# Computing an attention denominator from Gram sums of the key features, ahead of the numerator, in a fused linear-attention and FFN kernel

## Chip, cores and metric

One Trainium2 chip, one core of it. The metric is the device time in microseconds (us) of one launch. A run is called slow where it is over 1.5% above the fastest of the same kernel; comparisons below use fast runs, and where a run was slow the text says so.

Engine names in the profile: PE is TensorE (matmuls), PEld its weight loads, DVE is VectorE, ACT is ScalarE, POOL is GpSimd, SP is SyncE, which only issues DMAs here. SPq is SyncE's in-order queue of DMA issues.

## The reference

```python
# q, k, v: 4 batches x 4 heads x 1088 tokens x 32;  S1, S2: 8 x 32
def phi(x):                       # 64 features of a token: all products a_i * b_j
    a = einsum('rd,bhsd->bhsr', S1, x)
    b = einsum('rd,bhsd->bhsr', S2, x)
    return einsum('bhsi,bhsj->bhsij', a, b).reshape(..., 64)
q_p, k_p = phi(q), phi(k)
kv  = einsum('bhsf,bhsd->bhfd', k_p, v)
z   = sum(k_p, axis=2)
num = einsum('bhsf,bhfd->bhsd', q_p, kv)
den = einsum('bhsf,bhf->bhs', q_p, z)[..., None] + 1e-6
attn = num / den
x = attn.transpose(0, 2, 1, 3).reshape(4352, 128)      # 4 heads x 32 = 128 columns
h = maximum(x @ w_in, 0)                               # w_in: 128 x 2048
out = (h * h) @ w_out                                  # w_out: 2048 x 128
```

The point of the change: since phi is made of products, z is an 8 x 8 matrix, the Gram sum of a and b over the keys, and den = a_q' Z b_q. The denominator of a token needs only its 8 a-features and the 8 rows y = Z b_q (in this kernel the roles of a and b are laid out by the shuffles), not its 64 products.

## The kernel before

Tokens are handled in chunks: three per batch (384, 384 and 320 tokens), 12 in all. While TensorE runs the FFN of one chunk (16 steps: a matmul in f16 to 128 of the 2048 hidden columns, and an f32 matmul back, which the trace shows as two records), the other engines prepare the next chunk's attention. A small planner, run while the kernel is built, puts every attention task at one FFN step of one engine; the engines then run their instructions in exactly that order.

```python
def a_qg(b, ch):              # a and b features of q, packed 64x32 tiles
    for r in range(2):
        for o in range(4):
            nc.tensor.matmul(qg[32*o:32*o+32, 512*r : 512*r+n], sqn[...], qT[...])

def a_sh(b, ch, s, i):        # VectorE: spread features over partitions, 4 per chunk
    nc.vector.stream_shuffle(in_=qg..., out=t_..., mask=mask_q[s][i])

def a_qpn(b, ch, s):          # GpSimd: products of the features, read by a_ndn as they lie
    nc.gpsimd.tensor_tensor(out=qp, in0=sh0, in1=sh1, op=mult)

def a_ndn(b, ch):             # numerator (i = 0) and denominator (i = 1) rows
    for i in range(2):
        for g in range(2):
            for h in range(H):
                nc.tensor.matmul(nd[32*h:32*h+32, 512*g + 192*i : ... + n],
                                 kw[64*g:64*g+64, 128*i + 32*h : ... + 32],
                                 qpn[h % 2][64*g:64*g+64, c0 : c0 + n])
# then on VectorE, per chunk: a_dT (transpose of den), a_rd (reciprocal of 12 columns),
# a_rb (transpose back), a_x (num * 1/den); then ScalarE a_ax, TensorE a_sum,
# VectorE rs and s2 (a power-of-two scale per token), GpSimd a_xs -> xT, input of the FFN

class _Plan:
    LAG = {"PE": 2, "DVE": 1, "ACT": 1, "POOL": 1, "SP": 1}
    def add(self, key, eng, dur, needs, f, *args, ...):
        s = first
        for k in needs:
            s = max(s, self.at[k] + self.LAG[eng])     # steps after what it needs
        # ... then the first step with room on that engine; dur is an estimate in us
```

The FFN's own elementwise work (ReLU `gt`/`g` and squares `g`) is spread over ScalarE, VectorE and GpSimd by a balance that fills what the plan leaves free.

## Time and profile before

| | before |
|---|---|
| median of 4 runs | 194.94 us (194.86 to 195.44) |
| span of the profiled run | 193.2 us |
| TensorE busy | 185.9 us, 96% |
| VectorE / ScalarE / GpSimd busy | 122.8 / 138.1 / 94.7 us |

The page's first part: busy time of each engine, its share of the span, and its instructions.

```profile
span 193.2 us, 4586 instructions
PE 185.9 (96%) x1666; PEld 111.2 (58%) x1666; DVE 122.8 (64%) x316; ACT 138.1 (71%) x338; POOL 94.7 (49%) x158
```

The list of waits of TensorE before: engine and line, what it waited for, us in total, how many times, the longest.

```profile
PE warm L877 <- DVE zero L160: 1.2, 1, 1.2
PE pg L725 <- ACT xT L697: 0.3, 1, 0.3
PE xp L688 <- DVE xs L663: 0.3, 2, 0.2
PE pg L725 <- ACT gt L735: 0.2, 1, 0.2
```

All of that lies in the prologue, and it is about 2 us in sum. TensorE bounds the kernel, and what attention costs is the time that its matmul groups take between FFN steps. One such group, from the timeline of TensorE before (start us, duration, engine, line, operation, form, count):

```profile
94.39 0.70 PE L756 MATMUL po<-g,w_o 128*128 128x320 f32 x2
95.02 0.88 PE L472 MATMUL ndn<-qp,kw 64*32 64x192 f32 x32
95.69 0.53 PE L441 MATMUL qg<-qT,sqn 64*32 64x192 f32 x16
96.16 0.31 PE L725 MATMUL pg<-xT,w_in 128*128 128x320 f16 x1
```

Ends are modelled and overlap, so read starts. The FFN step in front of this group starts at 94.25, and a plain step of this chunk takes 0.675 us, so without the group the next step would have started at 94.93; it started at 96.16. The group costs 1.23 us. In this is a late start of the packed group of about 0.09 us (95.02 instead of 94.93).

### The profile page before, as it was taken

Reading aid. Unit: us, or ns where it says so; the run is one execution under the profiler, and the core shown is the slowest. Engines: PE = TensorE matmul, PEld = TensorE weight load, DVE = VectorE, ACT = ScalarE, POOL = GpSimd, SP = SyncE. Lnnn points to the kernel's source line nnn. Section 1 sums busy time; section 2 is a strip of 40 time slices with the busy share of each in tenths; the row PEclk is TensorE's granted clock in tenths of the full one; section 3 lists DMA queues with packets and bytes.
Section 4 is the critical chain, followed back from the end, with each engine's and each line's share of the span. In section 5 each row is a group of like instructions: output and inputs, shape, how many; then the busy total and the mean of one; then the engine's idle time right before and its main releaser. Section 6 shows DMA issues by size and latency. Waiting matters only on the chain.

```text
span 193.2 us, 4586 instructions
## 1 busy us (share of the span) xinstructions
PE 185.9 (96%) x1666; PEld 111.2 (58%) x1666; DVE 122.8 (64%) x316; ACT 138.1 (71%) x338; POOL 94.7 (49%) x158
## 2 busy tenths in 40 slices
PE   7998999999999999999999999999999999999990
PEld 2673655456656555456666555556566555556990
DVE  3958876974586763964566674873666665547740
ACT  3326695895496996996498896896596896867740
POOL 5833484955325382984346363984245371630000
PEclk9999999999999999999999999999999999999997
DMA  5699340020085100020157200010110200200201
GB/s 163 177 289 299 88 142 5 0 41 3 12 204 155 43 11 3 11 33 3 17 154 210 38 6 3 14 29 3 25 19 2 34 3 0 41 2 0 44 0 34
DMA packets 27344, 11.40 MB, mean 59 GB/s; under 512 B 19194, under 2 KB 26042, under 8 KB 27322
## 3 DMA queue, kind: packets, MB, share of 16 engines
q1 hardware_dynamic: 27174, 11.05, 23.5%
q8 instruction: 13, 0.21, 0.5%
q10 hardware_dynamic: 148, 0.07, 0.1%
q14 instruction: 9, 0.07, 0.1%
HBM read 8.78 MB, written 2.23 MB: 57 GB/s over the span
## 4 chain that ended last, share of the span: by engine, by line
PE 93%; DVE 2%; ACT 2%; issue 0%; DVEq 0%; ACTq 0%
PE po L756 58%; PE pg L725 16%; PE ndn L472 4%; PE kvp L338 2%; PE warm L877 2%; PE qg L441 2%; PE pt L773 2%; PE nd L595 2%; PE rep L901 1%; PE kvp L352 1%; PE sm L522 1%; PE kf L381 1%; PE kf L280 1%; ACT gt L735 1%; ACT g L719 1%
## 5 line engine op out<-in xcount | busy, mean ns | idle before, releaser
L756 PE MATMUL po<-g,w_o 128*128 128x384 f32 (+3 forms) x386 | 144.0, 459 | 0.0
L719 ACT ACTIVATE g<-gt 128x384 f32<-128x384 f32 (+1 forms) x164 | 80.7, 503 | 7.7 <-DVE gt L737 7.1
L735 ACT ACTIVATE gt<-pg 128x384 f32<-128x384 f32 (+2 forms) x137 | 64.6, 474 | 28.6 <-PE pg L725 27.9
L756 PEld LDWEIGHTS po<-g,w_o 128*128 128x128 f32 x386 | 65.9, 190 | 32.7 <-ACT g L719 18.7
L725 PE MATMUL pg<-xT,w_in 128*128 128x384 f16 (+2 forms) x193 | 60.9, 317 | 0.7 <-ACT xT L697 0.3
L737 DVE TENSOR_SCALAR gt<-pg 128x384 f32<-128x384 f32 (+1 forms) x56 | 29.4, 524 | 34.4 <-PE pg L725 27.9
L746 POOL TENSOR_TENSOR g<-gt 128x384 f32<-128x384 f32 (+1 forms) x26 | 20.7, 801 | 49.0 <-ACT gt L735 49.0
L725 PEld LDWEIGHTS <-w_in 128*128 128x128 f16 x193 | 18.9, 98 | 24.4 <-issue 6.8
L459 POOL TENSOR_TENSOR qp<-sh 128x384 f32<-128x384 f32 (+1 forms) x20 | 18.8, 948 | 7.9 <-DVE sh L450 7.9
L450 DVE STREAM_SHUFFLE sh<-qg 128x384 f32<-128x384 f32 (+1 forms) x40 | 20.4, 563 | 0.0
L546 POOL TENSOR_TENSOR xT<-x,rs 128x384 f16<-128x384 f32 (+1 forms) x10 | 9.5, 952 | 6.2 <-DVE rs L537 6.0
L306 POOL TENSOR_TENSOR kp<-fs 128x1152 f32<-128x1152 f32 x3 | 9.5, 3169 | 5.0 <-DVE fs L299 5.0
L537 DVE TENSOR_SCALAR rs<-sm 128x384 uint32<-128x384 uint32 (+1 forms) x10 | 5.3, 527 | 7.9 <-PE sm L522 7.9
L482 DVE STREAM_TRANSPOSE dT<-ndn 128x384 f32<-128x384 f32 (+1 forms) x10 | 5.5, 548 | 7.0 <-PE ndn L472 7.0
L788 POOL COPY br<-beta 32x3 f32<-32x3 f32 x32 | 5.9, 183 | 6.4 <-DVE beta L678 5.1
L472 PE MATMUL ndn<-qp,kw 64*32 64x192 f32 (+1 forms) x320 | 8.4, 318 | 0.0
L555 POOL TENSOR_TENSOR bt<-s 128x384 f32<-128x384 f32 (+1 forms) x10 | 7.9, 786 | 0.0
L472 PEld LDWEIGHTS ndn<-qp,kw 64*32 64x32 f32 x320 | 4.7, 106 | 4.9 <-issue 3.9
L364 POOL TENSOR_TENSOR ks<-kp 128x1024 f32<-128x1024 f32 x3 | 7.1, 2365 | 0.2
L877 PE MATMUL warm<-zero 128*128 128x512 f16 x16 | 5.7, 521 | 1.2 <-DVE zero L160 1.2
L338 PEld LDWEIGHTS kvp<-kp,vn 128*32 128x32 f32 x288 | 4.8, 110 | 2.7 <-issue 2.2
L274 DVE STREAM_TRANSPOSE qT<-qn 128x384 f32<-128x384 f32 (+1 forms) x12 | 6.3, 535 | 0.0
(119 smaller groups left out, 154.9 us busy)
## 6 DMA issues: line engine op xcount, KB each, us to landing
vn<-in_v_dram SPq DMA_DIRECT2D x32, 64.0 KB, 3.9
kn<-in_k_dram SPq DMA_DIRECT2D x3, 544.0 KB, 11.9
qn<-in_q_dram SPq DMA_DIRECT2D x3, 544.0 KB, 3.3
out_dram<-oT SPq DMA_DIRECT2D x24, 48.0 KB, 1.8
w_in<-in_moe_w_in_dram SPq DMA_DIRECT2D x2, 512.0 KB, 9.0
w_o<-in_moe_w_out_dram SPq DMA_DIRECT2D x2, 512.0 KB, 11.1
out_dram<-oT SPq DMA_DIRECT2D x12, 40.0 KB, 1.7
qn<-in_q_dram SPq DMA_DIRECT2D x2, 192.0 KB, 3.8
```

Of the source, the lines that this page charges most:

```text
L306: (nc.vector if g == 0 else nc.gpsimd).tensor_tensor(out=_ap(st[b, "kp2"], 0, 128, 128 * NT * g, [[64, 2 * NT], [8, 8], [1, 8]]), in0=_ap( ...
L450: nc.vector.stream_shuffle(in_=_ap(st[b, "qg", ch], 0, 128, 0, [[512, 2], [1, n]]), out=_ap(t_, 0, 128, 0, [[n, 2], [1, n]]), mask=mask_q[ ...
L459: nc.gpsimd.tensor_tensor(out=qp[:, 0 : 2 * n], in0=st[b, "sh", ch, s, 0][:, 0 : 2 * n], in1=st[b, "sh", ch, s, 1][:, 0 : 2 * n], op=mult,)
L472: nc.tensor.matmul(nd[32 * h : 32 * h + 32, 512 * g + 192 * i : 512 * g + 192 * i + n], st[b, "kw"][64 * g : 64 * g + 64, 128 * i + 32 * h ...
L546: nc.gpsimd.tensor_tensor(out=st[b, "xT"][:, 384 * ch : 384 * ch + n], in0=st[b, "x", ch][:, 0:n], in1=st[b, "rs", ch][:, 0:n], op=mult,)
L719: nc.scalar.activation(dst, src, Square)
L725: nc.tensor.matmul(pg[:, c0:c1], w_in[:, 128 * c : 128 * c + 128], st[b, "xT"][:, 384 * ch + c0 : 384 * ch + c1],)
L735: nc.scalar.activation(gt[:, c0:c1], pg[:, c0:c1], Relu)
L737: nc.vector.tensor_scalar(out=gt[:, c0:c1], in0=pg[:, c0:c1], scalar1=0.0, scalar2=None, op0=amax)
L746: (nc.vector if on[1] == "DVE" else nc.gpsimd).tensor_tensor(out=g2[:, c0:c1], in0=gt[:, c0:c1], in1=gt[:, c0:c1], op=mult)
L756: nc.tensor.matmul(st["po", b, ch][:, c0:c1], w_o[:, 128 * c : 128 * c + 128], g2s[i][1][:, c0:c1], start=first, stop=(c == NFF - 1), skip ...
L877: nc.tensor.matmul(t_[:, 0:512], zero[:, 0:128], zero[:, :])
```

## The change

Intent: take the denominator rows out of `ndn` (half its matmul records), replace the z matmuls (16 records of 64 columns a batch) by shorter Gram records (18 of 32 columns), and fold 1/den into the q features, so that the nd2 matmul gives x directly and the VectorE chain behind it (dT, rd, rb, x) goes. The feature order that the Gram form needs is not the order in which nd2 must read the products, so six SBUF-to-SBUF DMAs per chunk (`mv`) move them. Batch 0 keeps the old form; batches 1 to 3 (nine chunks) use the new one. Names below: nd2 is the new numerator group (tile `ndn`), qgy the matmuls of the q features and y rows (tile `qk`), kf those of the key features, kvp the group that sums over the keys; `xT` is the input of the FFN, `gt` its ReLU, `g` its square, and `xs`, `rs`, `s` the scaling of x. The core of the diff:

```diff
+    def a_gram(b, t):                       # 32-column Gram records instead of z
+        nc.tensor.matmul(kvp[32*(t%4):..., 64:96], fs[.. odd ..], fs[.. even ..], ...)
+    def a_qgy(b, ch, qg):                   # q features and y rows, 96 columns each
+    def a_shf(b, ch, e, s):                 # six 192-wide shuffles; those of e = 2 read qu
+    def a_pr(b, ch):                        # pr = q feature * y, transposed to tr
+    def a_den(b, ch):
+        nc.vector.tensor_reduce(out=dn, in_=tr, axis=AX, op=add)
+        nc.vector.tensor_scalar(out=de, in0=dn, scalar1=1e-6, op0=add)
+        nc.vector.reciprocal(rr[:, 96 columns], de[12 columns, each read 8 times])
+    def a_qu(b, ch):                        # rb = transpose(rr); qu = q feature * rb
+    def a_qp2(b, ch, e):                    # GpSimd: sha[e] * shb, for e = 0, 1
+    def a_mv(b, ch, e):
+        for q_ in range(2):
+            for to, of, w in ((0, 0, 32), (96, 32, 32)) if e == 0 else ((32, 0, 64),):
+                nc.sync.dma_start(ft[to : to+w, 384*q_ : ...], qp[64*q_ + of : ... + w, ...])
-                        st[b, "kw"][..., 128 * i + 32 * h : ...],      # i = 0, 1
-                        st[b, "qpn", ch, h % 2][...],
+                    st[b, "kw"][64*g : 64*g+64, 32*h : 32*h+32],       # a_nd2: one pass
+                    _ap(st[b, ch, "ft"], 64*g, 64, 192*(h%2) + 96*(h//2), [[384, 2], [1, 96]]),
     # plan, per chunk m of batches 1 to 3
+        nd_tasks(n, ch)              # nd2 of chunk m together with qgy of chunk m + 1
+        x_tasks(n, ch)               # x of chunk m: scale on VectorE, rs, xT, s2
+        feature_tasks(*divmod(m + 1, 3))   # yc, shuffles, den, qu, qp2, mv of chunk m + 1
+        P.at["mv", b, ch, 1] += 4    # nd2 at least that many steps after the last move
+    SKIP = (0, 1, 6, 11)             # tail: spread the skipped last-tile matmuls
```

## The prediction

> **What bounds the kernel now.** TensorE. The table of busy time by stretch has it busy throughout 20 to 172 us; the list of waits gives it under 2 us; the chain of waits is 93% TensorE. In the timeline one FFN step (a 384-column f16 and a 384-column f32 matmul) repeats every 0.81 us, every 0.675 us in a 320-column chunk. What counts is TensorE work inserted between steps. VectorE (64% busy), ScalarE (71%) and GpSimd (49%) matter only where TensorE waits for them.
>
> **Inserted TensorE work, from the timeline (start to start, with the about 0.09 us late start of each packed group).** ndn 192 columns + qg 192: 1.22 us; ndn + qg 160: 1.18; ndn 160 + kf: 1.29; qg alone: 0.58; the kvp group with z: 1.46; two transposes: 0.22; a sum matmul: 0.16. Each packed group costs about 0.27 us more than its columns stream (2 clocks a column, 8 or 4 tiles side by side). The Trainium skill, "TensorEngine Tiling (Array Packing)", Key Properties, says that changing the tiling mode drains TensorE; the 0.27 us agree in direction. From batch 0's last chunk on: 1.29 + 3 x (0.58 + 1.46 + 0.22) + 2 x 3.69 + 3.20 + sums 1.5 + 0.22 = about 20.4 us.
>
> **What changes there.** Half the ndn records go (the denominator rows): -0.32 us per 192-column chunk. qg keeps its columns but doubles with the new y rows; at 96 columns each, both together should stream in 0.32 us, if such short records still pack. qg of chunk 0 and kf join other groups, saving mode switches. The z matmuls (16 records of 64 columns, 0.21 us) become 18 Gram records of 32 columns (0.12). Estimates: nd2+qg+kf 1.40, nd2+qg 0.92, nd2 0.60, kvp 1.37 to 1.45, transpose plus the S2b matmul 0.4 (two weight loads of 0.18 us hide behind little), the split sum 0.2. Sum about 18.1 us: **-2.3 us**.
> Tail: the skipped last-tile matmuls are spread (steps 0, 1, 6, 11); the timeline shows some 0.4 us of stalls at 178 to 180 us, where they stood together: -0.3 us. One kvT moves into the prologue, behind warm-up matmuls.
>
> **What it adds elsewhere.** Per chunk, VectorE loses four 384-wide shuffles (0.56 us each), dT, de, rd, rb, x, and gains six 192-wide shuffles, pr, tr, three den operations, rb, qu and xs, in bursts of about 6 us over six steps (4 to 5 us). GpSimd loses ks1 and ks2 (4.4 us a batch) and xs, so more squares go to it (39 planned, 26 before). Six SBUF-to-SBUF DMAs per chunk enter the path to nd2; four output stores show about 1.9 us from issue to landing, and about six steps are left for the moves. Most is off the critical path; I expect one stall of about 0.4 us where xs of batch 1's first chunk is just in time, some tenths elsewhere: +0.4 to +0.9 us.
>
> **Sum.** 194.9 - 2.3 - 0.3 + 0.5 = about **192.7 us**, 8 in 10 within 191.0 to 194.6. Faster by over 2%: 0.12; within 2%: 0.85; slower: 0.03.
>
> **Right or wrong shows in:** TensorE busy throughout the middle; ndn records halved; nd2+qg near 0.92 us; kvp group not above 1.46; few TensorE waits on VectorE or DMA.
>
> **What would make it wrong:** 96-column records that don't pack (qg 0.7 us: +2 us in all); Gram column groups serializing the kvp group; nd2 waiting for the moves; VectorE bursts delaying ReLU or xs.

## The result

| | before | after |
|---|---|---|
| median | 194.94 us | 216.41 us (215.94 to 217.87, 4 runs) |
| ratio of fast runs | 1 | 1.1108, 95% interval 1.105 to 1.1167 |
| span of the profiled run | 193.2 us | 214.2 us |
| TensorE busy | 185.9 us | 190.0 us |

A ratio is the mean time of one kernel's fast runs over that of the kernel before in the same rounds, so it is not quite the ratio of the medians. The changed kernel is correct, and slower by 11%. The page's first part, after:

```profile
span 214.2 us, 4808 instructions
PE 190.0 (89%) x1684; PEld 113.5 (53%) x1684; DVE 131.7 (62%) x377; ACT 139.3 (65%) x348; POOL 86.6 (40%) x157
```

TensorE now idles. The largest three in the list of waits of TensorE, after:

```profile
PE ndn L642 <- DMA ft<-qp: 9.9, 6, 2.7
PE pg L913 <- DVE xT L733: 2.7, 2, 2.0
PE pg L913 <- DVE gt L925: 2.0, 3, 0.9
```

Six of the nine nd2 groups wait for the moves, and FFN matmuls wait for VectorE. All gaps over 0.02 us between TensorE instructions add up to 18.0 us, against 1.1 us before. The chain of waits shows why the moves are late. This is one turn of it, from one nd2 group to the next (start us, us, what; the last column names who did it; "..." marks pieces left out, and pieces of under 0.1 us are left out without a mark):

```profile
108.47 0.60 PE ndn L642 x12
109.06 0.34 PE qk L554 x21
...
111.49 0.93 DVE sha L577 x4
112.42 0.26 DVE pr L590
...
113.86 0.75 DVE rr L606
114.61 0.42 DVE rs L725
115.06 0.56 DVE xT L733
115.62 0.46 DVE s L717
...
116.80 0.66 DVE shb L582 x3
117.53 1.02 POOL qp L619
118.56 0.56 SPq L632
119.17 0.59 SPq L632
119.80 0.59 SPq L632
120.43 0.59 SPq L632
121.12 0.54 SPq L632
121.70 2.18 DMA ft<-qp
123.88 0.14 issue
124.02 0.60 PE ndn L642 x12
```

Read it as a sum: 3.0 us from the group's start until VectorE begins, 6.0 us of VectorE's burst (111.49 to 117.46; the work for the previous chunk's x, rs, xT and s, stands inside the burst), 1.0 us GpSimd, 3.1 us of five DMA issues of about 0.6 us in a row, and 2.2 us from the start of the sixth issue (121.70) to its landing, in all 15.55 us with the small steps between. The six issues by themselves take 3.7 us (118.56 to 122.30). It is a loop: the q features that start it come out of the same TensorE group as the nd2 that ends it. TensorE stood 2.03 us before the nd2 at 124.02. The eight intervals between the nine nd2 groups are 16.8, 16.8, 15.2, 15.6, 15.4, 14.9, 15.6 and 15.7 us, nearly alike although chunks differ in length; without the moves (first experiment below) they are 15.0, 16.8, 14.2, 13.4, 15.6, 13.2, 12.7 and 14.4.

There is a second cost. Twice the granted TensorE clock fell to one half for 3.4 us. The table by stretches after (window, then us and busy per engine, PEclk, DMA share, GB/s), around the first of them:

```profile
64.00:68.20 4.20, 2.15 (x10) 1.23 (x9) 4.02 (x13) 2.08 (x7) 0.74 (x1) 1.00 0.58 162
68.20:71.60 3.40, 3.40 (x9) 1.68 (x8) 1.43 (x5) 2.77 (x8) 2.04 (x3) 0.50 0.20 71
71.60:75.00 3.40, 3.40 (x15) 1.97 (x14) 2.95 (x5) 2.48 (x7) 1.92 (x1) 1.00 0.48 110
```

The stretch at 0.50 follows a wait of 2.05 us, for VectorE's `xT`, that ended at 66.97. The second one (170.6 to 174.0) follows the wait of 2.69 us for the moves that ended at 169.84. Together they stretch FFN steps by about 3 us. The Trainium skill, "TensorE: Matmul & The Clock Gate", "What's actually happening", describes a half-rate state after an idle window of about 3.4 us, with a free-running window. The state and its 3.4 us length agree with this trace; the threshold does not, for here 2.05 us of standing was enough once, while two other waits of 2.09 and 2.03 us (at 59.76 and 124.02) were not followed by it. Nor was a wait of 2.04 us at the same place in e1 (below), which ended at 64.46. What decides it I did not settle: three later profiles (e2, e4 and h3 below) show such a stretch at 19 to 20 us, at the end of the prologue, where no single gap just before it was over 0.35 us.

So the 21.0 us of added span are: about +17 us of gaps on TensorE, about +3 us at half clock, about -2 us of shorter TensorE groups (by the sum of terms near the end), and some 3 us in small steps that I did not itemise. One kind of them can be read from starts in e1 below: a step with a wait is in most cases about 0.16 us longer than a plain step and the listed wait together (1.62 us at 78.38, against 0.81 and 0.65).

### The profile page after: what moved, and what is told of

It reads as the page before. It is cut to its first block, busy times and chain, and to the rows that moved or that the text cites. A ratio compares the mean times of both kernels' runs of the same rounds, so it can differ in the third digit from the quotient of the medians.

```text
span 214.2 us, 4808 instructions
## 1 busy us (share of the span) xinstructions
PE 190.0 (89%) x1684; PEld 113.5 (53%) x1684; DVE 131.7 (62%) x377; ACT 139.3 (65%) x348; POOL 86.6 (40%) x157
## 4 chain that ended last, share of the span: by engine, by line
PE 56%; DVE 16%; SPq 7%; DMA 6%; ACT 5%; issue 4%; POOL 4%; ACTq 0%; DVEq 0%
PE po L944 30%; PE pg L913 9%; SPq L632 7%; DMA ft<-qp 6%; POOL qp L619 3%; DVE sha L577 3%; PE kvp L382 2%; PE ndn L642 2%; ACT gt L923 2%; PE warm L1065 2%; PE qk L554 2%; DVE rr L606 2%; PE pt L961 2%; DVE shb L582 1%; PE nd L783 1%
## 5 line engine op out<-in xcount | busy, mean ns | idle before, releaser
L923 ACT ACTIVATE gt<-pg 128x384 f32<-128x384 f32 (+2 forms) x148 | 69.7, 475 | 41.6 <-PE pg L913 39.6
L907 ACT ACTIVATE g<-gt 128x384 f32<-128x384 f32 (+1 forms) x151 | 74.8, 505 | 11.0 <-DVE gt L925 10.6
L934 POOL TENSOR_TENSOR g<-gt 128x384 f32<-128x384 f32 (+1 forms) x39 | 31.6, 816 | 44.9 <-ACT gt L923 43.6
L925 DVE TENSOR_SCALAR gt<-pg 128x384 f32<-128x384 f32 (+1 forms) x45 | 23.4, 526 | 16.0 <-PE pg L913 12.1
L619 POOL TENSOR_TENSOR qp<-sha,shb 128x384 f32<-128x384 f32 x18 | 17.6, 1000 | 9.9 <-DVE shb L582 9.9
L642 PE MATMUL ndn<-ft,kw 64*32 64x192 f32 x144 | 5.6, 332 | 9.9 <-DMA ft<-qp 9.9
L577 DVE STREAM_SHUFFLE sha<-qk 128x192 f32<-128x192 f32 x36 | 11.9, 371 | 0.0
L350 DVE TENSOR_TENSOR kp<-fs 128x1152 f32<-128x1152 f32 x3 | 8.7, 2889 | 0.0
L606 DVE RECIPROCAL rr<-de 128x96 f32<-128x96 f32 x9 | 6.8, 754 | 0.3
L382 PE MATMUL kvp<-kp,vn 128*32 128x64 f32 x288 | 6.4, 222 | 0.3 <-issue 0.3
```

The costliest lines, as they stand in the source:

```text
L350: (nc.vector if g == 0 else nc.gpsimd).tensor_tensor(out=_ap(st[b, "kp2"], 0, 128, 128 * NT * g, [[64, 2 * NT], [8, 8], [1, 8]]), in0=_ap( ...
L382: nc.tensor.matmul(st[b, "kvp"][32 * h : 32 * h + 32, 0:64], _ap(vn[b], 0, n, v0 + dv * h, [[1, 32]]), kp[0:n, at[h] : at[h] + 64], start= ...
L577: nc.vector.stream_shuffle(in_=q_ap(b, ch), out=two(st[b, ch, "sha"], 384 * e + 192 * s), mask=mask)
L619: nc.gpsimd.tensor_tensor(out=st[b, ch, "qp2"][:, 384 * e : 384 * e + 384], in0=st[b, ch, "sha"][:, 384 * e : 384 * e + 384], in1=st[b, ch ...
L642: nc.tensor.matmul(nd[32 * h : 32 * h + 32, 512 * g : 512 * g + 192], st[b, "kw"][64 * g : 64 * g + 64, 32 * h : 32 * h + 32], _ap(st[b, c ...
L907: nc.scalar.activation(dst, src, Square)
```

## The experiments

Theories at the start. **A**: the serial loop from the q features through VectorE, GpSimd and six moves to nd2 is longer than TensorE's work on a chunk, and the moves are its largest part that can be taken out. Rivals: **B**: VectorE's bursts (length and order) are the cause and the moves only show up last; **C**: the wider layout of the k features slows the products `kp` (2.9 us in the mean on VectorE after, 1.3 us before) and so the key side; **D**: the plan's estimates are wrong, so that the FFN's elementwise work sits in VectorE's bursts.

### 1. Take the moves away, shorten the chain, or both

Results wrong. `e1_no_moves`: nd2 reads the products where GpSimd wrote them.

```diff
-            for to, of, w in ((0, 0, 32), (96, 32, 32)) if e == 0 else ((32, 0, 64),):
+            for to, of, w in ():
-                    _ap(st[b, ch, "ft"], 64 * g, 64, ...
+                    _ap(st[b, ch, "qp2"], 64 * g, 64, ...
```

> The changed kernel without the six SBUF-to-SBUF DMAs of each chunk: nd2 reads the product tile itself (wrong result on purpose, same shapes, same order of everything else). Theory A (a serial chain from one chunk's qg to its nd2, which is as long as the chunk's FFN, makes TensorE wait; the moves are 5.3 us of its 15.6 us): the waits of ndn for ft (9.9 us in the profile, 11 us with what follows them) go, the half-clock stretches mostly go too, and the time falls by 9 to 14 us, to 202 to 207 us. Theory B (VectorE and GpSimd simply have too much work, and delay ReLU, squares and xT): the moves occupy neither, so under 4 us, 212 us or more. Theory C (TensorE's own added records cost more than estimated): no change, 216 us.

`e2_short_chain`: the last two shuffles read the q features instead of qu.

```diff
-                in_=st[b, "qu", ch][:, :], out=st[b, ch, "shb"][:, 192 * s : 192 * s + 192],
+                in_=q_ap(b, ch), out=two(st[b, ch, "shb"], 192 * s),
```

> The changed kernel with the scaled features' shuffle reading qg itself, so that products, sums, reciprocal and scaling (pr to qu) are still done in the same order on VectorE, but nothing waits for them (wrong result on purpose). VectorE is in order and runs the two shuffles at the same place, so theory A predicts little from the broken dependence alone: the shuffles stay behind the same VectorE instructions. If under 1.5 us is gained, VectorE's order, not the latency of its dependences, sets the length of this part of the chain; if over 4 us, the dependences do.

`e3_both` has both edits.

> Both of the former. Theory A: as without the moves, within 1.5 us of it.

| | us (range) | ratio to before [95%] |
|---|---|---|
| e1_no_moves | 204.57 (203.62 to 205.51) | 1.0494 [1.0372, 1.0616] |
| e2_short_chain | 215.26 (213.47 to 217.05; the profiled run slow) | none given |
| e3_both | 202.93 (202.68 to 203.17) | 1.041 [1.036, 1.046] |

The moves are worth about 12 of the 21.5 us. This includes the two half-clock stretches, which are gone in e1 (clock 0.994). The e2 edit does nothing that these runs can tell: its one fast run, 213.47, lies 2.5 us below the fastest of the changed kernel, and one run is not enough. In the same way e3 lies 1.6 us below e1, a little more than was expected, but the intervals overlap. It is a weak test: it removes a dependence, but the two shuffles still stand at the end of VectorE's in-order list, behind everything they used to depend on. The main waits that e1 leaves in TensorE's list:

```profile
PE pg L913 <- DVE gt L925: 2.9, 4, 0.9
PE pg L913 <- DVE xT L733: 2.7, 2, 2.0
PE pg L913 <- ACT g L907: 0.6, 1, 0.6
PE po L944 <- POOL g L934: 0.5, 2, 0.3
```

With the waits gone, e1 is also where TensorE's own cost can be read cleanly. The timeline of TensorE in e1, one nd2 group with the q features and y rows of the next chunk:

```profile
88.41 0.81 PE L944 MATMUL po<-g,w_o 128*128 128x384 f32 x2
89.15 0.56 PE L642 MATMUL ndn<-qp,kw 64*32 64x192 f32 x16
89.50 0.37 PE L554 MATMUL qk<-qT,sk 64*32 64x96 f32 x16
89.66 0.48 PE L554 MATMUL qk<-qT,sy 64*32 64x96 f32 x16
90.07 0.34 PE L913 MATMUL pg<-xT,w_in 128*128 128x384 f16 x1
```

The FFN step that starts at 88.25 is followed by one at 90.07: 1.82 us, less the 0.80 us of a plain step, gives 1.02 us for the group. The busy times of e1's page, for TensorE's work as a whole:

```profile
PE 185.7 (92%) x1684; PEld 110.7 (55%) x1684; DVE 131.4 (65%) x377; ACT 138.6 (69%) x348; POOL 86.6 (43%) x157
```

### 2. The layout of the k features alone

`e4_flat_fs` stores the k features in two flat halves, stride 2 instead of 4 (result wrong, since the Gram records then read the wrong columns).

```diff
-                _ap(st[b, "fs"], 0, 128, 2 * g, [[32, 2 * NT], [4, 8], [1, 2]]),
+                _ap(st[b, "fs"], 0, 128, 32 * NT * g, [[16, 2 * NT], [2, 8], [1, 2]]),
-            in0=_ap(fs, 0, 128, 2 * g, [[32, 2 * NT], [4, 8], [0, 8]]),
+            in0=_ap(fs, 0, 128, 32 * NT * g, [[16, 2 * NT], [2, 8], [0, 8]]),
```

> The changed kernel with the k features of the two halves kept apart, as before the change (strides of 2 elements, not 4), with the Gram matmuls reading the same tile at the same strides as in the changed kernel (wrong result on purpose). The VectorE products kp took 1.31 us before and 2.2 to 4.2 us after. If the layout is the reason, they take 1.3 us again and GpSimd's 2.2 to 3.1 us; theory B then expects 3 us or more to be gained, theory A under 2 us (kp delays one ReLU of 0.9 us and its following, in three places).

Measured 215.68 us (214.57 to 216.79), ratio 1.1064 [1.0922, 1.1206]. The VectorE products did get shorter (1.35, 1.37 and 2.75 us, against 2.21, 2.28 and 4.17 us after), but the kernel did not, as far as these runs tell. Theory C falls as a cause of the time: the key side has slack.

### 3. The tail alone

`e6_before_skip` is the kernel before with only the spread-out tail of the change.

```diff
     LAST = 4
+    SKIP = (0, 1, 6, 11)
-            if i >= NS - NFF + LAST:
-                ffn2_tile(i - LAST)
+            if i - (NS - NFF) not in SKIP:
+                ffn2_tile(i - sum(j <= i - (NS - NFF) for j in SKIP))
```

> The kernel before with only the tail part of the change (the last tile's matmuls left out at steps 0, 1, 6 and 11 of the last chunk and not at 0 to 3). Prediction: 0.3 us faster. Within 0.5 us in any case.

Measured 194.85 us, ratio 1.001 [0.9946, 1.0073]. The tail is worth nothing that shows outside this interval, six or seven parts in a thousand either way. The predicted 0.3 us is within that, so it is neither confirmed nor refuted.

### 4. The balance alone

`e8_balance_only` is the changed kernel, except that the balance of FFN work is told what the trace showed: 0.35 us more for the denominator operations, 0.9 us more for VectorE's `kp`.

```diff
+        for k_, s_ in P.at.items():
+            if k_[0] == "den":
+                load["DVE"][s_] += 0.35
+            if k_[0] == "kp" and k_[2] == 0:
+                load["DVE"][s_] += 0.9
```

> The changed kernel with only that correction of the two sizes. Theory A: TensorE waits for the moves anyway, so a ReLU that comes earlier is mostly given back at the next nd2: under 2 us gained. Theory B: 3 us or more.

Measured 215.72 us (215.53 to 219.6, the profiled run slow), ratio of fast runs 1.1035 [1.1, 1.107]: at most a fraction of a per cent. Theory D, in the form of these two estimates, does not carry the loss.

### 5. Break the loop: q features two chunks ahead

If the loop is the cause, its latency need not be shortened; it is enough to give it two chunks of TensorE work. `h1_two_ahead` changes the plan, not the work: the features of chunk m + 2 are made in the group of nd2 of chunk m. The result is correct. `h2_two_ahead_balance` adds the balance correction of experiment 4.

```diff
     for m in range(5, 3 * B):
         n, ch = divmod(m, 3)
-        nd_tasks(n, ch)                               # with q features of chunk m + 1
+        nd_tasks(n, ch, divmod(m + 2, 3) if more else None, kb, first=16 * m - 20)
         x_tasks(n, ch)
-        feature_tasks(*divmod(m + 1, 3))
+        feature_tasks(*divmod(m + 2, 3))
```

> The changed kernel, right result, with the plan changed so that the features qg of a chunk are computed two chunks before the chunk's nd2 shares a group with the next one (from the middle of batch 1 on; the first groups of batch 1 and the last two stand alone, which adds four mode switches, about +1.2 us). Nothing else is taken away: same moves, same VectorE work. Theory A (the loop from one group's qg through VectorE, GpSimd and the moves to the next group's nd2 takes 15.5 us, longer than the 14.2 us of TensorE work in a chunk): the waits of nd2 for the moves go except in batch 1's first one or two chunks, the half-clock stretches go, and the time falls to 202 to 208 us, near the run without moves. Theory B (too much VectorE and GpSimd work): under 3 us gained.

> The same, with the kernel's own choice of who does ReLU and square told the measured length of two VectorE pieces: the den group 1.2 us instead of 0.85, kp 2.3 instead of 1.36. If the waits of FFN matmuls for a ReLU on VectorE (2.0 us, and what follows) come from these sizes, 1 to 3 us less than the one before; if they come from VectorE bursts as such, no difference beyond 1 us.

h1: 213.52 us (213.09 to 215.0), ratio 1.0945 [1.0893, 1.0998]. h2: 212.3 us (212.1 to 213.85), ratio 1.0888 [1.0837, 1.0939]. Only 3 to 4 us better than after, where e1 says 12 are to be had; the 202 to 208 us that I expected of h1 did not come. The ranges of h1 and h2 overlap, so the balance correction is again not told from nothing. The list of waits of h1 names the reason. First TensorE's, then those of SyncE's queue:

```profile
PE ndn L642 <- DMA ft<-qp: 8.6, 3, 7.0
```

```profile
SPq L131 <- DVE qT L314: 20.8, 1, 20.8
```

One single nd2 group waited 7.0 us for its moves. The products had been ready since 89.23, but their moves stood in SyncE's in-order queue behind four output stores and a load of q for batch 3 (line 131), which waited 20.8 us for VectorE's last transposition out of the buffer that it overwrites. In my plan for h1 I had moved that load forward. The wait ran from 103.63 to 110.66; from 106.5 on, still inside it, the clock was at one half for 10.3 us (second column: the stretch's length; the value after the five engines' busy times is PEclk):

```profile
106.50:116.80 10.30, 6.14 (x61) 4.15 (x62) 2.35 (x13) 2.97 (x8) 0.00 (x0) 0.50 0.45 95
```

### 6. The same, with the load in its place; and moves on two queues

`h3_late_q_load` is h2 with only the place of that load changed.

```diff
-            at = 2 * i if n == 1 else s0 - 16 + 2 * i
+            at = 2 * i if n == 1 else 88 if (n, i) == (3, 4) else s0 - 16 + 2 * i
```

> The two-ahead version with corrected balance (212.3 us), with the load of q for batch 3 issued later, after the last transposition that reads the buffer it overwrites, so that it no longer holds up the queue of the moves. Result correct. Theory (the 7.0 us wait of nd2 of batch 2's first chunk and the 6.8 us at half clock after it came from that load standing ahead of the moves in SyncE's order): both go, 202 to 206 us, clock above 0.99. Rival (TensorE then waits elsewhere, because the VectorE bursts carry the loop): 208 to 212 us.

`h3n_late_q_no_moves` takes the moves out of h3 by the edit of e1 (wrong).

> As the late q load version, without the moves (nd2 reads the products where they lie; result wrong on purpose). If the lead of two chunks hides the moves: within 1 us of the late q load version. If they are still on the path: 2 to 4 us below it. In both cases what is left above the kernel before (195 us) belongs to VectorE's bursts and GpSimd, not to the moves; expected 200 to 204 us.

`m1_two_queues` is the changed kernel with half of the moves issued by GpSimd, `h3m_late_q_two_queues` is h3 with the same edit; both correct.

```diff
-                nc.sync.dma_start(
+                (nc.sync, nc.gpsimd)[q_].dma_start(
```

> The kernel after, with three of each chunk's six moves issued by GpSimd instead of SyncE; all else, and the result, as after. Theory (TensorE stands because the loop from the q features to nd2 is longer than the TensorE work of a chunk, and the six issues of about 0.59 us in a row are 3.5 us of that loop): the loop gets 1 to 1.5 us shorter, six waits get shorter by about that, so 208 to 212 us, and the waits of nd2 for the moves fall from 9.9 us to about 3 to 5. Rival (what delays is the landing of the data, about 2.2 us, or VectorE's burst, whoever issues the moves): 215 to 217 us. If the issue costs GpSimd more than SyncE it may be slower.

> As the late q load version, with three of the six moves issued by GpSimd. If moves still hold up nd2 in that version: 1 to 2 us below it. If with a chunk's lead the moves are off the critical path: the same within 1 us, or slightly slower because GpSimd has more to do.

| | us (range, 4 runs each) | ratio to before [95%] |
|---|---|---|
| h3_late_q_load | 204.28 (204.2 to 206.2) | 1.0453 [1.0374, 1.0533] |
| h3n_late_q_no_moves | 204.21 (202.86 to 204.91) | 1.0418 [1.0338, 1.0498] |
| m1_two_queues | 224.08 (223.52 to 225.81) | 1.1456 [1.1371, 1.1541] |
| h3m_late_q_two_queues | 216.95 (216.08 to 218.28) | 1.1062 [1.0975, 1.1149] |

h3 lies 8 us below h2 by the place of one load, and level with its twin without moves: with a lead of two chunks the moves are off the critical path, though every one of them is still made. In h3 the waits for moves are down from 9.9 us to

```profile
PE ndn L642 <- DMA ft<-qp: 1.5, 2, 0.8
```

Changed plan against changed work, the same 12 us: that settles theory A for this part of the loss. (h3 also has the balance correction of h2, which alone moved nothing that the runs can tell.)

m1 went the other way, and I had it wrong: I expected 208 to 212 us. TensorE's list of waits in m1:

```profile
PE po L944 <- POOL g L934: 7.7, 5, 2.6
PE ndn L642 <- DMA ft<-qp: 6.2, 2, 3.6
```

GpSimd was busy 14.8 us with issuing the moves, 0.55 us each in the mean, and while it issues it does not do its other work: the squares `g` of the FFN come late, and TensorE waits 7.7 us for them, which it did for only 0.2 us after. The profile of m1 also has four half-clock stretches of 3.4 us, two more than after. The waits for moves did fall, from 9.9 to 6.2 us, but since TensorE now stood elsewhere for 7.7 us this alone does not show that shorter issues shorten the loop; the cost was moved onto an engine with other urgent work. h3m shows the same: expected within 1 us of h3 or slightly slower, it came out 12.7 us slower, with waits of 8.4 us for the squares of GpSimd, 3.6 us for moves and two half-clock stretches. The Trainium skill, "DMA: Bandwidth & Descriptors", "SWDGE vs HWDGE vs iDMA", says that descriptors of DMAs issued from GpSimd are made by software there, and that the hardware path of SyncE sets up faster; the trace agrees only in that GpSimd is occupied (0.58 us for one issue, at 56.25 us of m1; SyncE took 0.54 to 0.60 us in the turn above, but has nothing else to do).

### 7. What is left: VectorE's bursts

e1, h3 and h3n all stand about 9 us above the kernel before. Their waits name VectorE (`xT`, `gt`, `s`), but a named wait is not yet a cause. `b1_light_burst` is e1, and `b2_two_ahead_light_burst` is h3n, with two of four `sha` shuffles taken out of each chunk's burst, and a shorter reciprocal (both wrong). The expectation counts about 1.2 us; by the starts in the timelines it is nearer 0.85 us, two shuffles at 0.28 us and 0.28 us of the reciprocal. The plan, the balance and the order are unchanged.

```diff
+        if e == 1:
+            return                                     # a_shf: shuffles of e = 1 left out
-            in0=st[b, ch, "sha"][:, 384 * e : 384 * e + 384],
+            in0=st[b, ch, "sha"][:, 0:384],
```

`h4_short_reciprocal` is h3 with the reciprocal edit alone; it is correct.

```diff
-        nc.vector.reciprocal(
-            _ap(rr[ch % 2], 0, 128, 1, [[16, 12], [2, 8]]), _ap(de, 0, 128, 0, [[1, 12], [0, 8]])
-        )
+        rc = wpool.tile([128, 12], F32, tag="rc", name="rc")
+        nc.vector.reciprocal(rc[:, :], de[:, :])
+        nc.vector.tensor_copy(
+            _ap(rr[ch % 2], 0, 128, 1, [[16, 12], [2, 8]]), _ap(rc, 0, 128, 0, [[1, 12], [0, 8]])
+        )
```

> The kernel after without the moves, and VectorE's burst made lighter: only two of the four shuffles of q features (the second product reads the first's), and the reciprocal taken of the 12 columns and then copied out, instead of 96 results per partition. About 1.2 us of the 6 us burst go; result wrong on purpose. If the bursts carry the rest: from 204.6 us (no moves alone) down to 200 to 202, and TensorE's waits for xT and gt of VectorE about halved. If only the plan's places matter: 204 to 205.

> The late q load version without moves (204.2 us), with the same lighter burst; result wrong on purpose. If the bursts carry the rest: 200 to 202 us. If only the plan's places matter, or the split groups on TensorE: 203.5 to 204.5.

> The late q load version (204.3 us) with only the reciprocal changed: 12 columns, then a copy to 96. Result correct. The reciprocal's 0.75 us should become about 0.2 + 0.2. If the bursts carry the rest: 203 to 204 us; otherwise 204 to 204.5, which 3 rounds can't tell from no change.

| | us (range, 4 runs each) | ratio to before [95%] | against |
|---|---|---|---|
| b1_light_burst | 200.37 (199.36 to 201.25) | 1.0227 [1.0146, 1.0308] | e1: 1.0494 |
| b2_two_ahead_light_burst | 198.56 (198.38 to 199.04) | 1.0145 [1.0066, 1.0223] | h3n: 1.0418 |
| h4_short_reciprocal | 202.31 (202.28 to 203.45) | 1.0342 [1.0271, 1.0413] | h3: 1.0453 |

Both light bursts give 4 to 6 us: about half of the rest, from a seventh of the burst (nine chunks of 0.85 us are 7.7 us). In b1 the waits on VectorE fell from 5.6 us (2.9 for gt, 2.7 for xT, above) to 2.4 us:

```profile
PE pg L917 <- DVE xT L737: 1.4, 1, 1.4
PE pg L917 <- DVE gt L929: 1.0, 2, 0.9
```

The groups of instructions by form, the reciprocal after (first fence) and the pair in h4 (second; us in all, then ns of one, then idle time before):

```profile
L606 DVE RECIPROCAL rr<-de 128x96 f32<-128x96 f32 x9 | 6.8, 754 | 0.3
```

```profile
L608 DVE COPY rr<-rc 128x96 f32<-128x96 f32 x9 | 2.2, 248 | 0.3
L607 DVE RECIPROCAL rc<-de 128x12 f32<-128x12 f32 x9 | 2.1, 228 | 0.3
```

It saves 0.28 us per chunk, nine times, on the engine with the longest part of the chain, and the kernel gains about 2 us: the ranges of the runs of h3 and h4 do not overlap, though the intervals of their ratios do. The gain is about the sum of the shortenings (9 x 0.28 = 2.5 us), as it would be for an operation in a serial path. Theory B is shown for 4 to 6 of the last 9 us, beside A and not in its place. What of the last 3 us in b2 belongs to what, I did not measure; the four mode switches that the two-ahead plan adds (1.2 us by the estimate in h1's expectation) may be part of it.

The best correct version of the new form is h4, 202.31 us: 14 us better than the change as it was made, and still 3.4% slower than the kernel before. No experiment pointed to a version that beats the kernel before.

## Why the prediction was wrong

It said 192.7 us (191.0 to 194.6) and 85% for "within 2%"; the result is 216.41 us. Point by point:

- **"What bounds the kernel now. TensorE."** Right for the kernel before.
- **TensorE work: "Sum about 18.1 us: -2.3 us."** Right term by term, but not seen in the whole. The terms, read in e1 at steps without a wait: nd2 with features and y rows 1.02 us (predicted 0.92), with the key features 1.51 (1.40), nd2 alone 0.59 (0.60), kvp group 1.48 (1.37 to 1.45), transpose with the S2b matmul 0.25 (0.4), a sum 0.15 (0.2). By the prediction's own counting that is 1.29 + 0.59 + 2 x 1.51 + 6 x 1.02 + 0.59 + 3 x (1.48 + 0.25) + 9 x 0.15 = 18.2 us. The Gram records gained nothing: the kvp group was to be "not above 1.46", which it was before, and is 1.48. And TensorE's busy time in e1 is 185.7 us, against 185.9 before, not 2.3 less: groups and steps that meet a wait are longer than the terms say (0.16 us a time, above), and the rest of the difference I did not itemise. The 96-column records do pack. The mode-switch cost on which the estimate rested (the Trainium skill, "TensorEngine Tiling (Array Packing)", Key Properties: changing the tiling mode drains TensorE) held in its direction: nd2 alone costs 0.59 us for 0.32 us of streaming (an estimate: its 16 records of 192 columns run eight side by side, as long as one record of 384 f32 columns, of which the timeline of e1 has two in 0.65 us), the same 0.27 us more as before.
- **"Tail ... -0.3 us."** Not shown: 1.001 [0.9946, 1.0073] for the tail alone.
- **"Six SBUF-to-SBUF DMAs per chunk enter the path to nd2; four output stores show about 1.9 us from issue to landing, and about six steps are left for the moves. Most is off the critical path ... +0.4 to +0.9 us."** This is the step that failed. The size of a landing was right (2.16 and 2.18 us on the chain; the Trainium skill, "DMA: Bandwidth & Descriptors", "Anatomy of one DMA — SWDGE (gpsimd) path", gives about 2.0 us fixed cost for the other path; the trace has nearly the same on this one). But I counted one landing, and the last move has five issues ahead of it, about 0.6 us each one after the other; and I compared the moves with a number of planned steps and not the whole loop with a chunk's TensorE time. The whole turn takes 15.55 us in the trace. The stall term measured about +17 us of gaps where the prediction had +0.4 to +0.9: by experiment the moves carry 12 us of the loss (with the two half-clock stretches) and VectorE's bursts 4 to 6 of the other 9; the last 3 us stay open.
- **"in bursts of about 6 us over six steps (4 to 5 us)".** The 6 us were exact (111.49 to 117.46), and I had written down that they do not fit into the steps they are planned for. I treated the overrun as slack on an engine at 64%. It stands in the loop, and FFN work queued behind it on the same engine waits for it: 5.6 us in e1.
- **"few TensorE waits on VectorE or DMA"** would have shown it right; the list has 9.9 and 4.7 us. **"nd2 waiting for the moves; VectorE bursts delaying ReLU or xs"** stood under what would make it wrong, and both came true. I gave "slower" 3%.
- Not foreseen at all: a halved clock after a wait of only 2 us.

## What to carry to other kernels

When a change inserts steps between a producer and a consumer on the bounding engine, add up the whole loop from that engine back to itself (each engine's burst, every DMA issue one after the other, and one landing) and compare it with the engine's work per turn; a share of busy time of 64% says nothing about it. If the loop is longer, lead by one more turn before you shorten anything, and look at what else stands in the in-order queues ahead of the loop's steps: one load issued too early cost 8 us here. Operations in the serial chain counted for more than half here (nine times 0.28 us gave about 2 us, nine times 0.85 us gave 4 to 6), and moving DMA issues to GpSimd, which had urgent work of its own, cost 8 to 13 us.

## What the Trainium skill lacked or had wrong

- "TensorE: Matmul & The Clock Gate", "Why this matters for your kernels": it asks only that no idle gap be over about 3 us. Here half clock for 3.4 us followed a single gap of 2.05 us (and one of 2.69 us), while gaps of 2.09 and 2.03 us, and one of 2.04 us in e1, were not followed by it. Around a 7.0 us wait it lasted 10.3 us, and three profiles had it at the end of the prologue with no gap over 0.35 us close before it. The page's section on psum-queue depth-cycling has frequent short idles bring the state on, but no length or number of them.
- "DMA: Bandwidth & Descriptors" has the fixed cost of a DMA, with about 50 ns for the sequencer's dispatch on the GpSimd path, but no time for which one issue holds the issuing engine: six issues in a row on SyncE took 0.54 to 0.60 us each; on GpSimd 27 took 0.55 us in the mean, during which its other work waited.
- No page that I found has the time of a VectorE reciprocal: 754 ns for 96 results per partition, 228 ns for 12.
- "SBUF — State Buffer" names a penalty for accesses that each go to a new 16-byte line, but neither it nor any page that I found has a time for a VectorE product of two SBUF operands at wider strides: 128 x 1152 in f32 took 1.31 us with features at stride 2 and 2.2 us at stride 4 (two of three; the third 4.17 us).
